# Sliding-window attention into a mixture of experts on one core: VectorE copy order, w2 rows in pairs, a fused sum and ReLU, and the order of tiles in the value matmuls

## The chip, the cores and the metric

The kernel runs on one core of one Trainium2 chip. The metric is the device time of one execution in microseconds (us); lower is better. Five engines take part: TensorE (PE; its weight loads are listed apart as PEld), VectorE (DVE), ScalarE (ACT), GpSimd (POOL) and SyncE (SP). Each has its own queue of instructions and works through it in order. POOL, SP and ACT also issue DMA transfers. Engines wait for each other by semaphores.

## The reference

The inputs are q, k and v for 4 batches, 8 heads, 768 positions and 64 values per head; routing weights for 3072 tokens and 4 experts; and for each expert w1 (512 x 1024) and w2 (1024 x 512). Cut to what matters:

```python
scores = scale * np.matmul(q, k.transpose(0, 1, 3, 2))
mask = np.where(retr, causal, causal & (is_sink | in_win))   # per head
a = softmax(np.where(mask, scores, -1e9))
x = np.matmul(a, v)             # laid out as 3072 tokens x 512
p = domain_probs / (domain_probs.sum(-1, keepdims=True) + 1e-09)
for e in range(E):
    h = np.maximum(x @ w1[e], 0.0)
    out += p[:, e:e + 1] * (h @ w2[e])
```

Heads 0, 2 and 6 attend to all earlier positions ("retrieval" heads); the other five attend to the first 4 positions and a window of 64.

## The kernel before, in words

**Attention in eight groups.** A group is one batch and one half of its 768 positions (`b`, `c`; group number `g` = 2b + c). `attention(b, c)` is a generator that emits the group's instructions step by step: transposed q and k, then per head `scores(h)` (key x query matmuls L659 into a PSUM bank, the exponential on ScalarE L677 into an `es` tile, and, except in group 0, a multiplication with a mask on VectorE L681) and `values(h)` or `values_r(h)` (value matmuls L785 and L713). The result goes to `xT`, the transposed tokens: 128 rows times 4 row blocks `ct` by 384 tokens. Heads with a window are scaled into `xT` by VectorE (L808) after a logarithm and an exponential on ScalarE (L803, L813). Retrieval heads go through `x_one` or `x_pair`, a transposition on TensorE (L762) and a copy by VectorE (L766, in `x_transposes`); in the later groups that copy is a DMA.

A retrieval head in the second half of a batch (`c` = 1) has four score tiles: the first two hold a diagonal block and are masked, the last two are not. `values_r` goes through them in the order in which `scores` made them (L705), and yields in the middle, after some 200 ns of matmuls (seven of them here).

**Instructions that wait their turn.** The order on each engine is written by hand. `later(op, g)` (L943) puts the scale L808 of a head into the list `behind`, due 1300 ns of estimated TensorE time later; `tick(ns)` (L946) moves that clock and emits what is due. In group 0 the end of the order is values of head 5 (row block 1), values of head 7 (row block 3), `x_transposes(6)` (all of row block 2), and then whatever is left behind. On VectorE this comes out as: scale of head 5, copy L766, scale of head 7.

**The experts.** Layer 1 multiplies w1 with the tokens, ReLU, and layer 2 multiplies with w2. Tokens of group 0 (three tiles of 128) and the first tile of group 1 go through `plain_steps`: for each expert L1027 takes 384 (or 128) columns of tokens against a 128 x 128 block of w1, over the row blocks in the order 0, 2, 1, 3. For the very first expert four PSUM banks are opened, and row blocks 0, 2, 1 are done for all four before row block 3. L1048 then multiplies with w2, 512 columns at a time.

The other tokens go in ten pairs of tiles through `pair_steps`. There layer 1 of the experts is plain (L1154, 256 columns), except for expert 3 always and expert 2 in the last three pairs: those take fewer products by a Strassen-Winograd scheme (`winograd_layer1`, L1183). In it `keep` copies a product to SBUF on ScalarE (L1193), and `add` adds a product in PSUM to a kept one on VectorE (L1199) and applies the ReLU in a second instruction (L1205); three such pairs for each expert and pair of tiles, 39 in all. Layer 2 of all pairs is L1290, with sums of w2 and of the hidden values made by VectorE (L967, L1134).

**The weights' way in.** All weights are cast from 4 to 2 bytes by DMAs that POOL issues: `load_w1(e, ...)` (L331, two DMAs of 64 partitions) and `load_w2(e)` (L339, one DMA). In `w2sb`, partition p holds rows p, 128 + p, 256 + p, ... of w2, one row of 512 to a block `ft`; the hidden unit that partition p of block `ft` of the hidden values stands for is therefore ft x 128 + p, and the weights of that block in layer 1 are 128 adjacent columns of `w1sb`. The loads go out in the order written in lines 491 to 527: w1 and w2 of expert 0, w1 of expert 1, then k and q for group 1 (L229), w2 of expert 1 and so on. `landed(x)` (L500) is a one-element copy on POOL that makes the instructions behind it wait until x has landed.

**Interleaving.** From group 1 on `moe_steps` emits the experts' work, and the loop at the end of the kernel inserts an attention step whenever a plan says so.

Of the kernel before, what the change touches and what calls it, by code (L numbers as in the profile page):

```python
# [9 lines left out]

# [3 lines left out]
ALU = mybir.AluOpType  # L14
# [4 lines left out]
def kernel(  # L19
# [33 lines left out]
    nc = tc.nc  # L53
    P = 128
# [276 lines left out]
    def load_w1(e, f0, f1):  # L331
        x = moe_w1[e].rearrange("(u c d) f -> u d c f", u=2, c=DMP)
        for u in range(2):
# [2 lines left out]
                in_=x[u, :, :, f0:f1],  # L336
            )

    def load_w2(e):  # L339
        gp.dma_start(  # L340
            out=w2sb[:, e * FTP : (e + 1) * FTP, :],
            in_=moe_w2[e].rearrange("(fo fi) d -> fi fo d", fi=P),
        )


    ONES = 0.0078125 * (1.0 + 15360.0 * 2.0**-23)
# [192 lines left out]
    def attention(b, c):  # L539
# [152 lines left out]
        def values_r(h):  # L692
# [9 lines left out]
            heads = heads.rearrange("p u (j x) -> p u j x", j=3)  # L702
            ps = heads[:, u if shared else 0, :, :]
            work = []
            for es, parts in es_of[h]:  # L705
                for t, o, q0, nq in parts:
                    for j in range(3):
                        x = j * P - q0
                        if 0 <= x < nq:
                            work.append((j, t, es[:, o + x : o + x + P]))  # L710
# [126 lines left out]
        if first:  # L837
# [17 lines left out]
            yield from both(scores(6), values(4))  # L855
            yield from both(scores(7), values(6))
            yield from values(5)
            yield from values(7)
            x_transposes(6)
            tick(LAG)  # L860
            small_things()
        else:
# [83 lines left out]
    def tick(ns):  # L946
        clock[0] += ns
        while behind and behind[0][0] <= clock[0]:
            behind.pop(0)[1]()
# [64 lines left out]
    def plain_steps(nt0, tiles, e, tokens, n0):  # L1014

        cols_n = tiles * P
        hs = hA[:, n0 : n0 + FTP * cols_n].rearrange("p (f x) -> p f x", f=FTP)
        require(nt0 // 3)
        x = tokens()
        ahead = 4 if nt0 == 0 and e == 0 else 1  # L1020
        for f0 in [0, *range(ahead, FTP)]:
            pss = {ft: bank() for ft in range(f0, f0 + (1 if f0 else ahead))}
            cts = (0, 2, 1, 3)

            def layer1(ft, n):
                ct = cts[n]
                nc.tensor.matmul(  # L1027
                    out=pss[ft][:, 0:cols_n],
                    lhsT=w1sb[:, e * DMP + ct, ft * P : (ft + 1) * P],
                    rhs=x[:, ct, :],  # L1030
                    start=(n == 0),
                    stop=(n == DMP - 1),
                )

            for ft in pss:
                for n in range(DMP - 1):
                    layer1(ft, n)
            for ft, ps in pss.items():
                layer1(ft, DMP - 1)
                nc.scalar.activation(  # L1040
                    out=hs[:, ft, :], in_=ps[:, 0:cols_n], func=AF.Relu
                )
                yield DMP * mm_ns(cols_n), 0.6
        for j in range(tiles):
            nt = nt0 + j
            ps_o = pO.tile([P, DM], FP32, name="pO", bufs=2)
            for ft in range(FTP):
                nc.tensor.matmul(  # L1048
                    out=ps_o,
                    lhsT=hs[:, ft, j * P : (j + 1) * P],  # L1050
                    rhs=w2sb[:, e * FTP + ft, :],
                    start=(ft == 0),
                    stop=(ft == FTP - 1),
                )
                if ft == FTP // 2 - 1:
                    yield FTP // 2 * mm_ns(DM), 1.4
            p_ap = p_sb[:, nt, e : e + 1]
            if e == 0:
                acc[nt] = acc_of(nt)
                nc.vector.tensor_scalar(  # L1060
                    out=acc[nt], in0=ps_o, scalar1=p_ap, scalar2=None, op0=ALU.mult
                )
            else:
                nc.vector.scalar_tensor_tensor(
                    out=acc[nt], in0=ps_o, scalar=p_ap, in1=acc[nt],
                    op0=ALU.mult, op1=ALU.add,
                )
            if e == E - 1:
                nc.sync.dma_start(out=out[nt * P : (nt + 1) * P, :], in_=acc[nt])
            yield FTP // 2 * mm_ns(DM), 1.4  # L1070
# [61 lines left out]
    def first_sum(e, n=1):  # L1132
# [2 lines left out]
            out=S1[:, k, :], in0=A21[:, k, :], in1=A22[:, k, :], op=ALU.add  # L1135
        )


    PSHARE = 1.57

# [5 lines left out]
    def pair_steps(nt0, nxt):  # L1146

        def plain_layer1(e):
            xs = scaled(e)
            for f0 in range(0, FTP, 2):  # L1150
                ps = bank()
                for f in range(2):
                    for ct in range(DMP):
                        nc.tensor.matmul(  # L1154
                            out=ps[:, f * PC : (f + 1) * PC],
                            lhsT=w1sb[:, e * DMP + ct, (f0 + f) * P : (f0 + f + 1) * P],
                            rhs=xs[:, ct, :],
                            start=(ct == 0),
                            stop=(ct == DMP - 1),
                        )  # L1160
# [15 lines left out]
        def winograd_layer1(e, x, y):  # L1176
# [18 lines left out]
            def block(n):  # L1195
                return blocks[:, n, e * HT : (e + 1) * HT, :]

            def add(n, ps, b):
                nc.vector.tensor_tensor(  # L1199
                    out=block(b),  # L1200
                    in0=ps.rearrange("p (f x) -> p f x", f=HT),
                    in1=kept[n].rearrange("p (f x) -> p f x", f=HT),
                    op=ALU.add,
                )
                nc.vector.tensor_scalar(  # L1205
                    out=block(b), in0=block(b), scalar1=0.0, scalar2=None, op0=ALU.max
                )

            def t(n):
# [337 lines left out]
```

The softmax here doesn't subtract the row's maximum and nothing guards it: scores larger than these inputs give would overflow.

## Time and profile before

| what | value |
|---|---|
| median of three runs | 378.41 us (377.46 to 378.68) |
| the profiled execution, its own time | 377.47 us |
| its span, first to last instruction | 375.8 us |
| mean granted TensorE clock | 1.000 |
| matmuls on L1154 (plain layer 1 of the pairs) | 864, 109.3 us busy |
| matmuls on L1290 (layer 2 of the pairs) | 1104, 133.4 us busy |
| first matmul of an expert (L1027) | at 20.37 us |
| transfers of w2, issue to landing, median of 4 | 12.5 us |
| packets in POOL's DMA queue | 86848 |

The profile is one execution of the program, taken by the hardware profiler. A row for a group of instructions gives its line, engine and operation, what it writes and reads, the shapes (partitions x elements, type) and how many there are, then its busy time and the mean length of one in ns, and last the idle time of the engine ahead of them with what ended most of it. A timeline row gives start and length in us. Matmuls are pipelined and each row of a matmul holds its full length, so matmuls overlap in the rows: the distance from one start to the next is the rate.

### The profile page before, as it was taken

How to read it: one execution, taken by the hardware profiler on the slowest of the kernel's cores; microseconds unless marked ns; L12 is line 12 of the kernel's file. 1: busy time of each engine (PE TensorE's matmuls, PEld its weight loads, DVE VectorE, ACT ScalarE, POOL GpSimd, SP SyncE). 2: the span in 40 equal slices, each digit the busy share in tenths (PEclk: the TensorE clock that was granted, in tenths of full speed). 3: DMA queues.
4: the chain of work that ended last, by engine and by line, in shares of the span. 5: the costliest groups of instructions: out<-in, count | busy, mean ns of one | idle time of the engine just before them, and what ended most of it. 6: DMA issues, size and time to landing. Idle time of an engine off the chain costs nothing.

```text
span 375.8 us, 10137 instructions
## 1 busy us (share of the span) xinstructions
PE 367.5 (98%) x4128; PEld 310.2 (83%) x4128; DVE 282.7 (75%) x620; ACT 227.8 (61%) x475; POOL 113.7 (30%) x155
## 2 busy tenths in 40 slices
PE   8889999999999999999999999999999999999996
PEld 4745466668998988999989898998899998999996
DVE  7774768697888679878758858967778868769572
ACT  3863478547785785765676955784777361450630
POOL 8934573882058038115601650320000000000000
PEclk9999999999999999999999999999999999999999
DMA  9999999999699599977904991951220300300101
GB/s 164 155 201 206 196 187 191 181 207 105 97 109 144 106 96 120 152 116 58 207 10 59 170 157 21 127 127 14 69 72 2 107 9 0 114 2 6 54 2 56
DMA packets 124771, 39.24 MB, mean 104 GB/s; under 512 B 113728, under 2 KB 118404, under 8 KB 124724
## 3 DMA queue, kind: packets, MB, share of 16 engines
q0 software_dynamic: 86848, 19.01, 59.1%
q1 hardware_dynamic: 36276, 19.18, 21.9%
q8 instruction: 32, 0.52, 0.6%
q10 hardware_dynamic: 1600, 0.39, 0.5%
q14 instruction: 15, 0.12, 0.1%
HBM read 44.89 MB, written 6.34 MB: 136 GB/s over the span
## 4 chain that ended last, share of the span: by engine, by line
PE 87%; DMA 7%; POOL 3%; DVE 2%; issue 0%; POOLq 0%
PE pO L1290 31%; PE pA L1154 25%; PE pO L1183 9%; DMA w2sb<-in_moe_w_dram 7%; PE pO L1048 6%; PE pA L659 5%; PE pA L1027 5%; PE pV L713 2%; PE pV L785 2%; PE pA L1183 2%; POOL vS L309 1%; POOL vR L303 1%; DVE xs L1112 1%; PE pA L1380 0%; POOL early L453 0%
## 5 line engine op out<-in xcount | busy, mean ns | idle before, releaser
L1290 PEld LDWEIGHTS <-hA 128*128 128x128 f16 x1104 | 104.9, 98 | 12.2
L1154 PE MATMUL pA<-xs,w1sb 128*128 128x256 f16 x864 | 109.3, 272 | 0.0
L1154 PEld LDWEIGHTS <-w1sb 128*128 128x128 f16 x864 | 80.7, 98 | 8.5
L1163 ACT ACTIVATE hA<-pA 128x512 f16<-128x512 f32 x108 | 64.4, 598 | 35.1 <-PE pA L1154 32.9
L1290 PE MATMUL pO<-w2sb,hA 128*128 128x256 f16 x640 | 76.7, 272 | 0.0
L677 ACT ACTIVATE es<-pA 128x384 f16<-128x384 f32 (+2 forms) x122 | 59.2, 511 | 27.1 <-PE pA L659 23.3
L305 POOL DMA_DIRECT2D vS<-in_v_dram x30 | 29.6, 989 | 111.7 <-PE pV L785 110.5
L1290 PE MATMUL pO<-tsb,hA 128*128 128x256 f16 x464 | 56.7, 272 | 0.0
L1112 DVE TENSOR_TENSOR xs<-xT,pB 128x1024 f16<-128x1024 f16 (+1 forms) x52 | 49.4, 969 | 1.2 <-DMA out_dram<-o 1.2
L967 DVE TENSOR_TENSOR hA<-hA 128x1024 f16<-128x1024 f16 x60 | 39.6, 684 | 0.4
L1040 ACT ACTIVATE hA<-pA 128x384 f16<-128x384 f32 (+1 forms) x64 | 22.2, 385 | 19.8 <-PE pA L1027 19.6
L1027 PE MATMUL pA<-xT,w1sb 128*128 128x384 f16 (+1 forms) x256 | 30.9, 273 | 1.3 <-DVE xT L766 0.8
L1048 PE MATMUL pO<-w2sb,hA 128*128 128x512 f16 x128 | 30.7, 379 | 0.3 <-DMA w2sb<-in_moe_w_dram 0.3
L1310 ACT COPY s<-pO 128x256 f32<-128x256 f32 x31 | 11.5, 372 | 27.7 <-PE pO L1290 21.9
L1027 PEld LDWEIGHTS <-w1sb 128*128 128x128 f16 x256 | 19.3, 98 | 10.2 <-issue 1.9
L808 DVE TENSOR_TENSOR xT<-pV,rc 64x384 f16<-64x384 f32 x37 | 20.5, 555 | 9.1 <-ACT rc L813 6.6
L1183 PEld LDWEIGHTS <-w1sb 128*128 128x128 f16 x416 | 26.3, 98 | 1.1 <-issue 0.2
L803 ACT ACTIVATE rc<-pV,eps 64x384 f32<-64x384 f32 x37 | 21.3, 576 | 6.5 <-PE pV L785 5.9
L1199 DVE TENSOR_TENSOR hA<-pO,s 128x512 f16<-128x512 f32 x26 | 17.9, 687 | 9.3 <-PE pO L1183 6.7
L681 DVE TENSOR_TENSOR es<-es,mS 128x384 f16<-128x384 f16 (+1 forms) x40 | 13.7, 343 | 13.4 <-ACT es L677 13.4
L659 PE MATMUL pA<-qT,kR 128*128 128x384 f16 (+2 forms) x120 | 22.9, 278 | 0.6 <-DVE kR L576 0.6
L1193 ACT COPY s<-pO 128x512 f32<-128x512 f32 x39 | 22.5, 585 | 1.4 <-PE pO L1183 1.2
(144 smaller groups left out, 498.2 us busy)
## 6 DMA issues: line engine op xcount, KB each, us to landing
pB<-p_rows SPq DMA_DIRECT2D x10, 512.0 KB
out_dram<-o SPq DMA_DIRECT2D x19, 256.0 KB
w1sb<-in_moe_w_dram POOLq DMA_DIRECT2D x8, 512.0 KB, 9.3
w2sb<-in_moe_w_dram POOLq DMA_DIRECT2D x4, 1024.0 KB, 12.5
vS<-in_v_dram POOLq DMA_DIRECT2D x30, 112.0 KB, 4.2
k_rows<-in_k_dram POOLq DMA_DIRECT2D x18, 128.0 KB, 5.6
q<-in_q_dram POOLq DMA_DIRECT2D x18, 128.0 KB, 6.4
vR<-in_v_dram POOLq DMA_DIRECT2D x24, 48.0 KB, 5.8
```

The source lines that it names most:

```text
L305: gp.dma_start(out=t[:, :, own_v(h)], in_=windows_of(v, b, h, c))
L659: nc.tensor.matmul(out=ps[:, o : o + nq], lhsT=key_tile(b, c, h, t), rhs=qTs[b, c][:, hp, q0 : q0 + nq], start=(n == 0 or not first), stop ...
L677: nc.scalar.activation(out=es[:, 0:cols], in_=ps[:, 0:cols], func=AF.Exp, scale=SC)
L967: nc.vector.tensor_tensor(out=out, in0=a, in1=b, op=ALU.subtract)
L1027: nc.tensor.matmul(out=pss[ft][:, 0:cols_n], lhsT=w1sb[:, e * DMP + ct, ft * P : (ft + 1) * P], rhs=x[:, ct, :], start=(n == 0), stop=(n = ...
L1048: nc.tensor.matmul(out=ps_o, lhsT=hs[:, ft, j * P : (j + 1) * P], rhs=w2sb[:, e * FTP + ft, :], start=(ft == 0), stop=(ft == FTP - 1),)
L1112: nc.vector.tensor_tensor(out=o, in0=xin, in1=pb.to_broadcast([P, DMP, n, P]), op=ALU.mult)
L1154: nc.tensor.matmul(out=ps[:, f * PC : (f + 1) * PC], lhsT=w1sb[:, e * DMP + ct, (f0 + f) * P : (f0 + f + 1) * P], rhs=xs[:, ct, :], start= ...
L1163: nc.scalar.activation(out=blocks[:, b0 : b0 + 2, k0 : k0 + 2, :].rearrange("p t f x -> p f t x"), in_=ps.rearrange("p (f t x) -> p f t x" ...
L1183: nc.tensor.matmul(out=ps[:, f * P : (f + 1) * P], lhsT=w[:, ct, f * P : (f + 1) * P], rhs=a[:, ct, :], start=(first and f == 0 and ct == ...
L1193: nc.scalar.copy(out=kept[n], in_=ps)
L1290: nc.tensor.matmul(out=ps, lhsT=a[:, k, :], rhs=b(k), start=(first and k == 0), stop=(k == KT - 1), skip_group_check=not first,)
```

## The change

Four edits, in all heads or experts that they name:

- **Copy order.** At the end of group 0, the scale of head 5 is taken out of the list `behind` and emitted after the copy of `x_transposes(6)`. On VectorE the order becomes copy L766, scale of head 5, scale of head 7. TensorE's and ScalarE's orders stay.
- **Two rows per partition.** For experts 0 and 1, w2 is loaded so that partition p of blocks 2m and 2m + 1 holds the adjacent rows 256m + 2p and 256m + 2p + 1. A piece of the transfer is then two rows, 4 KB read and 2 KB written, instead of one. The hidden units are thereby renumbered within each pair of blocks, and the weights of a block in layer 1 become every second one of 256 columns of `w1sb`. The loads of w1 stay as they are.
- **Fused sum and ReLU.** `add` in `winograd_layer1` is one instruction, min(sum, largest fp32 number) followed by max with 0, in place of two.
- **Unmasked tiles first.** For `c` = 1, `values_r` takes the third and fourth score tile first, and then the first and second.

```diff
+from concourse.dve_ops import TENSOR_ADD_SAT
...
+    def in_pairs(e):
+        return e < 2
+
+    def w1_tile(e, ct, ft):
+        x = w1sb[:, e * DMP + ct, :]
+        if in_pairs(e):
+            x = x[:, ft // 2 * 2 * P : (ft // 2 + 1) * 2 * P]
+            return x.rearrange("p (x j) -> p j x", j=2)[:, ft % 2, :]
+        return x[:, ft * P : (ft + 1) * P]
+
     def load_w2(e):
-        gp.dma_start(
-            out=w2sb[:, e * FTP : (e + 1) * FTP, :],
-            in_=moe_w2[e].rearrange("(fo fi) d -> fi fo d", fi=P),
-        )
+        x = w2sb[:, e * FTP : (e + 1) * FTP, :]
+        if in_pairs(e):
+            gp.dma_start(
+                out=x.rearrange("p (m j) d -> p m (j d)", j=2),
+                in_=moe_w2[e].rearrange("(m p j) d -> p m (j d)", p=P, j=2),
+            )
+            return
+        gp.dma_start(out=x, in_=moe_w2[e].rearrange("(fo fi) d -> fi fo d", fi=P))
...
-            for es, parts in es_of[h]:
+            tiles = es_of[h] if c == 0 else es_of[h][2:] + es_of[h][:2]
+            for es, parts in tiles:
...
             yield from values(5)
-            yield from values(7)
+            at_once = behind.pop()
+            v_steps = values(7)
+            yield next(v_steps)
             x_transposes(6)
+            at_once[1]()
+            yield from v_steps
             tick(LAG)
...
-                    lhsT=w1sb[:, e * DMP + ct, ft * P : (ft + 1) * P],
+                    lhsT=w1_tile(e, ct, ft),
...
-                            lhsT=w1sb[:, e * DMP + ct, (f0 + f) * P : (f0 + f + 1) * P],
+                            lhsT=w1_tile(e, ct, f0 + f),
...
+    LARGEST = 3.4028234663852886e38
...
             def add(n, ps, b):
-                nc.vector.tensor_tensor(
+                nc.vector._custom_dve(
+                    TENSOR_ADD_SAT,
                     out=block(b),
                     in0=ps.rearrange("p (f x) -> p f x", f=HT),
                     in1=kept[n].rearrange("p (f x) -> p f x", f=HT),
-                    op=ALU.add,
-                )
-                nc.vector.tensor_scalar(
-                    out=block(b), in0=block(b), scalar1=0.0, scalar2=None, op0=ALU.max
+                    s0=LARGEST,
+                    s1=0.0,
                 )
```

## The prediction

> **What bounds the kernel now.** I read the busy shares first, then TensorE's own waits, then the chain of waits around them in order of time, then the timeline of the two places where TensorE waits, then the transfers behind them, and last the rows of the operations that the change touches.
>
> ```profile
> ## 1 busy us (share of the span) xinstructions
> PE 367.5 (98%) x4128; PEld 310.2 (83%) x4128; DVE 282.7 (75%) x620; ACT 227.8 (61%) x475; POOL 113.7 (30%) x155
> ```
>
> TensorE is busy 98% of the span. Busy is not yet full rate, so I checked the rate: a piece of 32 matmuls over 128 columns takes 1.95 us with one matmul's 219 ns at its end, so they follow each other every (1.95 - 0.219)/31 = 55.8 ns, and eight of 256 columns take 0.87 us in the chain, 109 ns each. At 2.4 columns per ns (128 more columns, 53 ns more) that is the full rate of a granted clock of 1.000. Only instructions that make TensorE stand still, or make a matmul follow later than that, can move the end. This is the list of what TensorE's matmuls waited for (total us, times, longest):
>
> ```profile
> PE pA L1027 <- DVE xT L766: 0.8, 1, 0.8
> PE pV L713 <- DVE es L681: 0.6, 1, 0.6
> PE pA L1027 <- DMA w1sb<-in_moe_w_dram: 0.4, 1, 0.4
> PE pO L1048 <- DMA w2sb<-in_moe_w_dram: 0.3, 1, 0.3
> ```
>
> All four lie between 20 and 44 us; from 44 us to the tail TensorE's idle time is nil. The change aims at three of them. The chain of waits for 10 to 45 us (start, length, what):
>
> ```profile
> 13.13 12.54 DMA w2sb<-in_moe_w_dram
> ...
> 26.25 12.52 DMA w2sb<-in_moe_w_dram
> ...
> 38.81 1.02 PE pO L1048 x4
> ```
>
> So before 38.81 the chain is not TensorE's. It runs through the transfer of w2 of expert 0 into that of expert 1. The timeline at the two joints:
>
> ```profile
> 19.68 0.34 PE L762 MATMUL pV<-ident,x_pair 128*128 128x128 f16 x3
> 20.31 0.56 DVE L808 TENSOR_TENSOR xT<-pO,rc 64x384 f16<-64x384 f32 x1 [0.69 <-ACT rc L813]
> 20.37 0.32 PE L1027 MATMUL pA<-xT,w1sb 128*128 128x384 f16 x1 [0.36 <-DMA w1sb<-in_moe_w_dram]
> 20.90 0.56 DVE L766 CAST xT<-pV 128x384 f16<-128x384 f32 x1
> 21.52 5.45 PE L1027 MATMUL pA<-xT,w1sb 128*128 128x384 f16 x31 [0.82 <-DVE xT L766]
> 33.37 0.20 PEld L560 LDWEIGHTS <-q 128*64 128x64 f16 x6 [0.32 <-DMA q<-in_q_dram]
> ```
>
> **Copy order.** The copy L766 has its input at 20.02 (19.68 + 0.34), but stands behind the scale L808 of head 5, which waits for ScalarE until 20.31. In front, it runs at about 20.06 to 20.62; the scale follows at the spacing of these rows (20.90 - 20.31 = 0.59), 20.65 to 21.21. The scale of head 7 waited for ScalarE until 21.43 anyway, so it is not later. TensorE needs, in order, x rows 0, 2, 1: the first is there at 20.37, the second (the copy) at 20.65, the third (head 5's scale) at 21.25. Before, the third matmul ran at 21.52 + 0.16 = 21.68. Gain in the first layer: 21.68 - 21.25 = 0.43 us. No DMA is moved. Head 5's scale is what is now late.
>
> **Where that gain goes.** It must get past two landings. At 33.37 the weight load L560 waited for q, which lies in the Pool queue behind w1 of expert 1. Before 38.81 TensorE had taken in its 384-column matmuls by 38.35 (four from 37.70, 0.1625 us each; the list counts 0.28 of the rest as idle, as the last one drains until 38.53) and waited for w2 of expert 1. With all transfers unmoved, 0.43 us earlier only lengthens that wait from 0.46 to 0.89: **the copy order alone is worth 0.** What counts is how much earlier the two w2 transfers land.
>
> **w2 in pairs of rows.** The queue's packet count is one per contiguous piece: w2 of an expert is 1024 pieces of 1 KB (written), and becomes 512 of 2 KB. The bytes stay. The same queue, with 1 KB pieces of w2 of expert 0 (21 to 25 us), with 2 KB pieces of w1 (41.5 to 44.5) and with 1 KB pieces of w2 of expert 2 (47 to 50):
>
> ```profile
> DMA packets 743, 0.80 MB, mean 199 GB/s; under 512 B 13, under 2 KB 702, under 8 KB 742
> DMA packets 327, 0.63 MB, mean 210 GB/s; under 512 B 20, under 2 KB 20, under 8 KB 327
> DMA packets 623, 0.62 MB, mean 208 GB/s; under 512 B 15, under 2 KB 623, under 8 KB 623
> ```
>
> 1.049 MB at 199 is 5.27 us, at 210 it is 5.00, at 208 it is 5.04. So a transfer saves from 0.04 us (if 208 is what 1 KB pieces can do) to 0.27. The two rows for 1 KB disagree; between them I take 0.15 each, as the first is for expert 0 itself but has dips that need not come from the pieces. [...]
>
> Both transfers lie in one queue in order, so q lands 0.15 earlier and w2 of expert 1 0.30 earlier, at 38.48. TensorE, with 0.43 in hand and held to 0.15 of it at L560, is ready at 38.20 and starts L1048 at about 38.51: **gain 0.30**. On Pool the issue of w2 (908 ns, w1's of a quarter of the pieces 632) may shrink by up to 0.2; the queue is full then, so this is 0. Later landings (w1 of expert 2 seen at 46.97, needed at 47.80) move with the queue and keep their slack.
>
> **Unmasked tiles first.** L713 at 43.56 waited 0.57 for the masks on VectorE. In the new order its first seven matmuls take tiles 2 and 3 instead. By the row of three exponentials from 42.65 (1.47 us), tile 2 is ready at about 43.25 and tile 3 at 43.64; seven matmuls at 34 ns then end at about 43.76, against 43.56 + 0.24 = 43.80 before. I take **0.05**. From below: tile 3 is now the last needed, and a queued ScalarE row of 0.6 us before it would cost up to 0.5; from above: the whole 0.57. In the later groups other matmuls stand between, and TensorE's list has no wait for L681 or L677 there.
>
> **Fused sum and ReLU.** 39 instructions of 298 ns leave VectorE, 11.6 us:
>
> ```profile
> L1199 DVE TENSOR_TENSOR hA<-pO,s 128x512 f16<-128x512 f32 x26 | 17.9, 687 | 9.3 <-PE pO L1183 6.7
> L1205 DVE TENSOR_SCALAR hA<-hA 128x512 f16<-128x512 f16 x39 | 11.6, 298 | 1.3
> L1027 PEld LDWEIGHTS <-w1sb 128*128 128x128 f16 x256 | 19.3, 98 | 10.2 <-issue 1.9
> L557 PEld LDWEIGHTS pA<-early,hA 128*128 128x128 f32 x24 | 2.6, 144 | 1.3 <-POOL early L449 0.8 <-ACT es L677 0.3
> 73.86 1.95 PE L1027 MATMUL pA<-xT,w1sb 128*128 128x128 f16 x32
> ```
>
> The new operation is in no row. It reads the same PSUM bank, so between 687 ns (the plain add) and 985 (add and ReLU together); I take 687. Either way the end does not move: the cover is the matmuls of layer 1, and TensorE waits for none of these 39. Without cover (a product that goes on accumulating into the bank being read) the cost is what the add exceeds some 1.3 us of other matmuls by, so nothing up to 985 ns. Value **0**.
>
> **Strided weights.** w1 of experts 0 and 1 is now loaded every second column: 640 loads at L1154 under 109 ns matmuls, 64 at L1027 under 162 ns, 64 under 55.8 ns. No load in the trace is strided. A gain is excluded, as the load is already hidden. Lower end 0: the 98 ns of a load is latency, they pass every 55.8 ns. Upper end by the slowest load there is, the 4-byte one of L557: six of them in 0.67 us, (0.67 - 0.144)/5 = 105 ns apart. That still hides under 109 and 162 and costs 64 x (105 - 55.8) = 3.1 us. If nothing overlapped, 144 ns each, it would be 640 x 35 + 64 x 88 = 28 us. I take 0, since only the step changes and the type (2 bytes) and the 128 columns stay those of the 98 ns row. [...]
>
> **Sum.** 0.30 + 0.05 + 0 + 0 = 0.35 us off the profiled execution's 377.47 (span 375.8 and 1.7 around it, which stay). That execution is the lowest of its kind; the median is 378.41, so I predict 378.41 - 0.35 = 378.06, about **378.1**. What a measurement can tell from no change is some 0.3%, 1.13 us.
>
> **Rivals.** (1) *The packets do not matter*: 208 GB/s is the limit for either size, the w2 landing stays, and copy order is absorbed there. For it: w2 of expert 2. Against: w2 of expert 0. 378.41 - 0.08 - 0.05 = 378.3. (2) *The transfers gain more*: if a piece costs by its share of engine time (121% at 1 KB, 112% at 2 KB in those windows), a transfer saves 8% of 5.27, 0.43 us, two 0.86; then the copy's 0.43 passes L560, TensorE is ready at 37.92 as w2 lands (38.78 - 0.86), and with all of 0.57 at L713 it is 1.43: 377.0. Against: bytes per second differ by 5%, not 8. (3) *The strided load outlasts a 128-column matmul*: at L1027 with 128 columns, from 74 us on, price 3.1 - 0.35 = 2.75, so 381.2; it decides once a load takes more than 55.8 + 1500/64 = 79 ns, which the 98 ns duration does not rule out. (4) *A new wait at L713* for the last exponential in each of the four second groups, at most 4 x 0.5 = 2: 380.1; against it, the matmuls between.
>
> **Chances.** Forecast 0.38, (1) 0.17, (2) 0.23, (3) 0.18, (4) 0.04. The likeliest one's own range is 377.6 to 378.5 (0.04 to 0.27 per transfer, 0 to 0.3 at L713). The range takes in (2) and half the way to (3): 376.9 to 380.2. Faster 0.24 (case 2, and a little of the forecast), same 0.54, slower 0.22 ((3) and (4)).
>
> **What would show it.** L766 ahead of L808 on VectorE, TensorE's third L1027 near 21.25; 1024 packets fewer in the queue; L1048 of expert 1 near 38.5, still just behind its transfer; L1205 gone; L1154 still 109 ns apart and the 128-column L1027 still 1.95 us for 32. It is wrong if those 32 take more than 2.5 us, or if L1048 of expert 1 starts at 38.8 or before 38.2.

## The result, and the profile after

The changed kernel takes 378.12 us (median of 4 runs, 377.49 to 378.32) against 378.36 (4 runs, 377.46 to 378.68) for the kernel before, measured alongside it: a ratio of 0.9995, interval 0.9974 to 1.0016. No difference can be told, and the forecast was 378.1. The profiled execution took 378.03 us with a span of 376.3; the one of before took 377.47 with 375.8. So in this pair of traces the changed kernel is the longer one, though nearly every stage starts earlier in it. A later measurement with more runs gave 377.96 (11 runs, 377.51 to 379.93) against 377.50 (15 runs): 1.0010, interval 0.9997 to 1.0024. Two of the eleven executions of a later kernel, `pairs_rounds`, the profiled one among them, took 545.34 and 639.65 us at granted clocks of 0.657 and 0.560 and are left out of everything below.

In the changed kernel the line numbers are: L676 scores, L694 exponential, L698 mask, L732 value matmuls, L785 the copy and L827 the scale on VectorE, L1050 and L1071 the plain layers 1 and 2, L1179 layer 1 of the pairs, L1208 the Winograd products, L1225 the fused instruction.

The page of the changed kernel, busy shares and queues (packets, MB, share of 16 engines):

```profile
span 376.3 us, 10100 instructions
PE 368.0 (98%) x4128; PEld 310.6 (83%) x4128; DVE 271.6 (72%) x581; ACT 228.0 (61%) x475; POOL 113.2 (30%) x155
q0 software_dynamic: 85824, 19.01, 59.7%
```

VectorE loses 39 instructions and 11.1 us of work; TensorE is at 98% as before. POOL's queue has 86848 - 85824 = 1024 packets fewer at the same bytes. Its list of TensorE's waits (total us, times, longest):

```profile
PE pV L732 <- ACT es L694: 1.3, 2, 1.0
...
PE pO L1071 <- DMA w2sb<-in_moe_w_dram: 0.5, 1, 0.5
PE pA L1050 <- DVE xT L827: 0.3, 1, 0.3
PE pA L1050 <- DMA w1sb<-in_moe_w_dram: 0.3, 1, 0.3
```

The 0.8 us for the copy has become 0.3 us for the scale, and the wait for w2 has grown from 0.3 to 0.5. The wait for the masks is gone, but one for the exponential stands in its place: of the 1.3 us, 1.0 was there before (in group 0), 0.31 is new. The timeline of the changed kernel at the first matmul of an expert:

```profile
20.06 0.56 DVE L785 CAST xT<-pV 128x384 f16<-128x384 f32 x1 [0.44 <-PE pV L781]
20.27 0.72 PE L1050 MATMUL pA<-xT,w1sb 128*128 128x384 f16 x2 [0.25 <-DMA w1sb<-in_moe_w_dram]
20.65 0.56 DVE L827 TENSOR_TENSOR xT<-pO,rc 64x384 f16<-64x384 f32 x1
21.26 0.97 PE L1050 MATMUL pA<-xT,w1sb 128*128 128x384 f16 x5 [0.27 <-DVE xT L827]
```

The copy runs first, the scale directly behind it, and the third matmul starts at 21.26 (21.68 before). And the chain of waits of the changed kernel further on:

```profile
13.14 12.28 DMA w2sb<-in_moe_w_dram
...
26.00 12.55 DMA w2sb<-in_moe_w_dram
...
38.59 1.02 PE pO L1071 x4
```

The chain still runs through both transfers of w2, and L1071 of expert 1 still starts just behind its transfer, now at 38.59 instead of 38.81. The first transfer is 0.26 us shorter from issue to landing, the second 0.03 longer. So 0.22 us are gained at this point, and 0.24 at the first pair of tiles (L1179 starts at 87.90, before at 88.14). 0.14 of that is lost between 103 and 119 us, and at the end only 0.09 is left: VectorE's last instruction ends at 373.11 instead of 373.20. From there to the end of the span it is 3.2 us, where it was 2.6 before; that is where the longer span comes from. It is not chance. The last 32 matmuls and the next-to-last sum on VectorE, before:

```profile
370.92 1.95 PE L1380 MATMUL pA<-tsb,hA 128*128 128x128 f16 x32
372.09 0.29 DVE L1387 TENSOR_TENSOR o<-pA,s 128x128 f32<-128x128 f32 x1 [0.54 <-PE pA L1380]
```

and in the changed kernel:

```profile
370.83 1.95 PE L1405 MATMUL pA<-tsb,hA 128*128 128x128 f16 x32
372.35 0.29 DVE L1412 TENSOR_TENSOR o<-pA,s 128x128 f32<-128x128 f32 x1 [0.89 <-PE pA L1405]
```

The matmuls are the same, but the sum starts 1.52 us after the first of them instead of 1.17, and the span ends 5.47 us after it instead of 4.84. The runs below show the longer end in every kernel with the fused instruction and in no other.

The place of the loss, value matmuls of the second half of batch 1 (group 3), in the timeline of before:

```profile
116.92 1.47 ACT L677 ACTIVATE es<-pA 128x512 f16<-128x512 f32 x3 [0.49 <-PE pA L659]
...
118.19 0.38 PE L713 MATMUL pV<-vR,es 128*128 128x65 f16 x7
```

and in that of the changed kernel:

```profile
116.68 1.47 ACT L694 ACTIVATE es<-pA 128x512 f16<-128x512 f32 x3 [0.49 <-PE pA L676]
...
117.95 0.52 PE L732 MATMUL pV<-vR,es 128*128 128x65 f16 x7
```

Three exponentials in a row end at 118.15. In the old order the seven matmuls that start at 117.95 (0.24 earlier than before) would not touch the last of them; in the new order some of the seven need it, and they take 0.52 us instead of 0.38, although the row, being one group of seven, lists no wait.

### The profile page after: what moved, and what is told of

Same layout as the page of the kernel before. It is cut to its first block, busy times and chain, and to the rows that moved or that the text cites. A ratio compares the mean times of both kernels' runs of the same rounds, so it can differ in the third digit from the quotient of the medians.

```text
span 376.3 us, 10100 instructions
## 1 busy us (share of the span) xinstructions
PE 368.0 (98%) x4128; PEld 310.6 (83%) x4128; DVE 271.6 (72%) x581; ACT 228.0 (61%) x475; POOL 113.2 (30%) x155
## 3 DMA queue, kind: packets, MB, share of 16 engines
q0 software_dynamic: 85824, 19.01, 59.7%
HBM read 44.89 MB, written 6.34 MB: 136 GB/s over the span
## 4 chain that ended last, share of the span: by engine, by line
PE 87%; DMA 7%; POOL 3%; DVE 1%; issue 0%; ACT 0%; POOLq 0%
PE pO L1315 31%; PE pA L1179 25%; PE pO L1208 9%; DMA w2sb<-in_moe_w_dram 7%; PE pO L1071 6%; PE pA L676 5%; PE pA L1050 5%; PE pV L732 2%; PE pV L804 2%; PE pA L1208 2%; POOL vS L310 1%; POOL vR L304 1%; DVE xs L1135 1%; PE pA L1405 0%; POOL early L470 0%
## 5 line engine op out<-in xcount | busy, mean ns | idle before, releaser
L1179 PE MATMUL pA<-xs,w1sb 128*128 128x256 f16 x864 | 109.3, 273 | 0.0
L1179 PEld LDWEIGHTS <-w1sb 128*128 128x128 f16 x864 | 80.7, 98 | 8.5
L694 ACT ACTIVATE es<-pA 128x384 f16<-128x384 f32 (+2 forms) x122 | 59.2, 511 | 27.3 <-PE pA L676 23.5
L1050 PE MATMUL pA<-xT,w1sb 128*128 128x384 f16 (+1 forms) x256 | 31.1, 273 | 0.7 <-DVE xT L827 0.3
L1071 PE MATMUL pO<-w2sb,hA 128*128 128x512 f16 x128 | 30.7, 379 | 0.5 <-DMA w2sb<-in_moe_w_dram 0.5
L827 DVE TENSOR_TENSOR xT<-pV,rc 64x384 f16<-64x384 f32 x37 | 20.5, 555 | 9.8 <-ACT rc L832 7.3
L1050 PEld LDWEIGHTS <-w1sb 128*128 128x128 f16 x256 | 19.4, 98 | 9.7 <-issue 1.5
L1208 PEld LDWEIGHTS <-w1sb 128*128 128x128 f16 x416 | 26.3, 98 | 1.1 <-issue 0.2
L1225 DVE CUSTOM_DVE_ANT_0 hA<-pO,s 128x512 f16<-128x512 f32 x26 | 17.7, 689 | 12.5 <-PE pO L1208 8.8
L698 DVE TENSOR_TENSOR es<-es,mS 128x384 f16<-128x384 f16 (+1 forms) x40 | 13.7, 344 | 15.0 <-ACT es L694 15.0
L676 PE MATMUL pA<-qT,kR 128*128 128x384 f16 (+2 forms) x120 | 22.9, 278 | 0.6 <-DVE kR L593 0.6
```

Source lines behind the costliest of these rows:

```text
L676: nc.tensor.matmul(out=ps[:, o : o + nq], lhsT=key_tile(b, c, h, t), rhs=qTs[b, c][:, hp, q0 : q0 + nq], start=(n == 0 or not first), stop ...
L694: nc.scalar.activation(out=es[:, 0:cols], in_=ps[:, 0:cols], func=AF.Exp, scale=SC)
L1050: nc.tensor.matmul(out=pss[ft][:, 0:cols_n], lhsT=w1_tile(e, ct, ft), rhs=x[:, ct, :], start=(n == 0), stop=(n == DMP - 1),)
L1071: nc.tensor.matmul(out=ps_o, lhsT=hs[:, ft, j * P : (j + 1) * P], rhs=w2sb[:, e * FTP + ft, :], start=(ft == 0), stop=(ft == FTP - 1),)
L1179: nc.tensor.matmul(out=ps[:, f * PC : (f + 1) * PC], lhsT=w1_tile(e, ct, f0 + f), rhs=xs[:, ct, :], start=(ct == 0), stop=(ct == DMP - 1),)
L1208: nc.tensor.matmul(out=ps[:, f * P : (f + 1) * P], lhsT=w[:, ct, f * P : (f + 1) * P], rhs=a[:, ct, :], start=(first and f == 0 and ct == ...
```

## The experiments

The questions: is the gain 0.22 us a matter of the packets (my theory) or of when the transfers happen to land; is the copy order really worth nothing alone; and what does the order of tiles cost? All runs compute the full result. To compare executions whose first transfers land at different times, I use distances between two starts. "First layer" is the distance from the start of the normalization of the pair's values (`x_pair`, VectorE) to the first layer-2 matmul of expert 0: 7.54 us in the trace of before. "Group 3" is the distance from the start of layer 2 of the first pair (L1290, at 103.85 us before) to the start of layer 1 of the next pair (L1154, at 118.62), around the place shown above: 14.77 us before, 14.91 after. "End" is the distance from the first of the last 32 matmuls to the end of the span: 4.84 us before, 5.47 after.

### The kernel before once more (`before_again`)

No edit.

> The kernel before once more, to see how much one profiled execution differs from another at the marks that the other runs are read by: first layer 1 of expert 0 in full flow at 21.52 us, q of group 1 landed at 33.13, L1048 of expert 1 at 38.81, first L1154 at 88.14, last matmul piece at 370.92. If these marks move by more than 0.1 us without any edit, differences of 0.2 us between traces say nothing. I expect 0.05 us or less on TensorE's and VectorE's marks, up to 0.2 us on landings of transfers, and up to 0.7 us between the last VectorE instruction and the end of the span (2.6 us before, 3.2 in the changed kernel).

Measured: 377.85 us, span 376.1 (378.15 for the other run of the same kernel beside it). The times agree, but not the stages. The first matmul of an expert starts at 21.26 instead of 20.37. The transfers as POOL saw them land, in the first trace of before:

```profile
20.29 0.18 POOL L502 COPY seen<-w1sb 1x1 f16<-1x1 f16 x1 [1.46 <-DMA w1sb<-in_moe_w_dram]
25.80 0.23 POOL L502 COPY seen<-w2sb 1x1 f16<-1x1 f16 x1 [3.76 <-DMA w2sb<-in_moe_w_dram]
33.15 0.18 POOL L502 COPY seen<-q 1x1 f16<-1x1 f16 x1 [6.01 <-DMA q<-in_q_dram]
```

and in this one:

```profile
21.17 0.18 POOL L502 COPY seen<-w1sb 1x1 f16<-1x1 f16 x1 [2.34 <-DMA w1sb<-in_moe_w_dram]
26.98 0.20 POOL L502 COPY seen<-w2sb 1x1 f16<-1x1 f16 x1 [4.06 <-DMA w2sb<-in_moe_w_dram]
34.20 0.18 POOL L502 COPY seen<-q 1x1 f16<-1x1 f16 x1 [5.88 <-DMA q<-in_q_dram]
```

Identical code lands its weights 0.9 to 1.2 us apart, and the layer 2 of expert 1 starts 0.38 us apart (38.81, 39.19). My expectation was missed by a wide margin: a difference of 0.22 us between two traces is below what one execution differs from the next. The distances hold: first layer 7.55, group 3 14.78, end 4.83.

### The copy order alone (`copy_only`)

```diff
-            yield from values(7)
-            x_transposes(6)
+            at_once = behind.pop()
+            v_steps = values(7)
+            yield next(v_steps)
+            x_transposes(6)
+            at_once[1]()
+            yield from v_steps
```

> Only the copy order. Theory (what the forecast rests on): the first layer gains 0.43 us (third L1027 at 21.25 instead of 21.68) and the wait for w2 of expert 1 swallows all of it, so that matmul row stays at 38.81 +- 0.1 with a gap ahead of it about 0.4 us longer, and the first L1154 stays at 88.1. Rival: the copy order itself brought the 0.22 us that the changed kernel shows there (38.59), because the landing of w2 has nothing to do with its pieces; then it reads 38.6 here too.

Measured: 377.34 us, span 375.6. First layer 7.13, so 0.41 us shorter. But the second half of my expectation fell. Part of the chain of waits of this run:

```profile
20.79 0.56 DVE xT L766
21.38 0.57 DVE xT L808
21.99 1.96 PE pA L1031 x11
...
38.09 0.76 PE pA L1031 x4
38.84 0.86 PE pO L1052 x4
```

No transfer is in it: here w2 of expert 1 had landed, and layer 2 followed layer 1 without a wait. From the start of expert 0's layer 2 to expert 1's it is 11.56 us, against 12.01 before and 12.21 after, both of which contain a wait for w2. `later_t` below has the old order and no wait for q or w2 there either: it needs 19.16 us from `x_pair` to layer 2 of expert 1, `copy_only` 18.69. So the copy order's gain reaches this point when q and w2 land in time, and is swallowed, as in the changed kernel's first trace, when they don't.

### The pairs of rows alone (`pairs_only`, `pairs_rounds`)

The edits to `load_w2`, `w1_tile` and the two places that use it, nothing else.

> Only w2 of experts 0 and 1 in pairs of rows, with the strided weights. Theory: w2 of expert 0 lands 0.25 us earlier (25.42 in the changed kernel, 25.67 before), L1048 of expert 1 starts near 38.6, as with the whole change, since TensorE is ready at 38.35 without the copy order too; so pairs alone bring all of the 0.22 us. Rival: the landings vary by that much from run to run, and the start is anywhere between 38.5 and 38.9. The strided loads cost nothing by the changed kernel's rows (98 ns, 128-column matmuls 1.95 us for 32): the same is expected here.

Measured in one execution: 380.59 us, span 378.9. Group 0 was late (first layer 1 at 21.32) and w1 of expert 2 landed at 48.89 instead of 46.97. Between 44 and 90 us TensorE waited 1.3 us for w1 (of experts 2 and 3) and 0.4 for w2; another 0.5 us went near 250 us. Nothing in the edit touches the load of w1, and `tiles_only`, with the old loads, has it as late as 48.31. So the same kernel was timed in more executions:

> The kernel with only w2 of experts 0 and 1 in pairs of rows, again and timed in five rounds, since its one look gave 380.59 us where the kernel before gave 378.15 on the same chip and where the whole change gave 378.12. Theory: the 2 us are one slow stretch of transfers (w1 of expert 2 landed at 48.89 us instead of 46.97, with TensorE waiting), as w1 of expert 0 landed 0.9 us apart in two executions of the same kernel; so five rounds give a median within 0.4 us of the kernel before (377.9 to 378.8). Rival: the strided weights or the larger pieces cost 2 us unless the other three edits come with them; then the median is 380 or more.

Measured: 377.52 us (median of 9) against 377.46 (33 runs): 1.0003, interval 0.9992 to 1.0014. None of the nine is above 378.55, so the 2 us of the first execution are not the kernel's. The edit is worth nothing that can be measured in the time; the strided loads cost nothing either, unless a gain of the loads hides it.

For the transfer itself, the time from the landing of w1 of expert 0 to that of w2 of expert 0, by POOL's copies: with one row to a piece 5.51, 5.81, 5.31, 5.54, 6.34, 5.69, 5.47 and 5.70 us in eight executions; with two rows 5.36, 5.08, 5.24 and 5.23 in four. The middle values are 5.62 and 5.24. That speaks for some 0.4 us less: only one of the eight (5.31) is below the longest of the four. But the eight spread over 1 us, so the size is uncertain.

### The order of tiles alone (`tiles_only`), and the change without it (`no_tiles`)

```diff
-            for es, parts in es_of[h]:
+            tiles = es_of[h] if c == 0 else es_of[h][2:] + es_of[h][:2]
+            for es, parts in tiles:
```

> Only the order of tiles in the value matmuls. Theory from the changed kernel's trace: nothing gained at group 1 (L1048 that follows at 43.8, within 0.05), and 0.14 us lost at group 3, where the seven value matmuls near 118.2 take 0.52 us instead of 0.38 as they wait for the exponential of the last tile; so the pair that begins at 149.34 before begins at 149.5. Rival: the 0.14 is a side effect of the other edits having moved the attention steps, and is not there alone: 149.34.

Measured: 379.0 us, span 377.3. Group 3 is 14.91, as in the changed kernel. The rest of its extra time lies elsewhere: a late w1 (0.8 us of waits) and a wait of 0.7 us near 249 us that is told of below.

> The whole change without the order of tiles in the value matmuls. Theory: the seven value matmuls of group 3 take 0.38 us again instead of 0.52, so the stretch from the second to the third stage of the pairs (103.6 to 118.6) is 14.77 us as before, not 14.91, and the time is 0.13 us lower than the whole change, 377.9 to 378.1 in the median; nothing is lost at group 1. Rival: the masks then hold up group 1 by 0.2 us or more (L713 there waited 0.57 for VectorE before), and the time is that of the whole change or higher.

Measured: 377.45 us, 1.0002, interval 0.9993 to 1.0011, span 375.7. Group 3 is 14.78 again. Over all runs the distance is 14.77 to 14.78 in every kernel of before's order (`before_again`, `copy_only`, `pairs_only`, `no_tiles`, `ct_major`, `halves` and both `reorder` runs) but `later_t`, which waits for q there, and 14.91 in every one of the new order (the change twice, `tiles_only`). So the new order costs 0.14 us there, each time. What it gains is in group 1, where the changed kernel has:

```profile
42.43 1.47 ACT L694 ACTIVATE es<-pA 128x512 f16<-128x512 f32 x3 [0.21 <-PE pA L676]
43.08 0.65 PE L732 MATMUL pV<-vR,es 128*128 128x65 f16 x7 [0.31 <-ACT es L694]
43.57 0.81 PE L1071 MATMUL pO<-w2sb,hA 128*128 128x512 f16 x3
```

Layer 2 at 43.57 is 4.98 us behind the start of expert 1's layer 2 (38.59). Before, it was 43.80 - 38.81 = 4.99. The matmuls start 0.48 us earlier, but four of the seven run and the other three then stand until the exponential of the second unmasked tile is done: 0.01 us gained.

`no_tiles` also shows where a gain at the front goes in the time. Its first pair starts at 87.73 us (88.14 before) and its last 32 matmuls at 370.53 (370.92), so it is still 0.39 us ahead there. But its end is 5.17 us, 0.33 more than before's 4.84, and the span comes out 0.06 shorter. The end is 4.83 or 4.84 in the ten traces without the fused instruction, among them `copy_only`, `pairs_only` and `tiles_only`, and 5.17, 5.47 and 5.25 in the three with it (`no_tiles` and the change twice). In these three the next-to-last sum on VectorE starts 1.51 to 1.53 us after the first of the 32 matmuls, in the ten 1.16 or 1.17. The fused instruction was not run alone, so a combination of it with the copy order or the pairs isn't excluded. Why the sum is late is open. One thing differs nearby: the last 8 KB packet of the DMA queue that the page calls instruction (q14) lies 2.8 to 3.0 us ahead of the end in the three and 23 to 30 us in the ten. It starts behind the late sum, so it can't be what delays that; what it does to the output transfers was not tested.

### The first layer row block by row block (`ct_major`), and the weights in halves (`halves`)

With the copy order, the opening of the first expert goes through the row blocks outermost, so that the four banks' work on block 0 and block 2 covers the scale that is late:

```diff
-            for ft in pss:
-                for n in range(DMP - 1):
+            for n in range(DMP - 1):
+                for ft in pss:
                     layer1(ft, n)
```

> Copy order, and besides the first layer of expert 0 takes row block 0 for all four open banks, then row block 2, then 1, instead of 0, 2, 1 bank by bank, so that the four matmuls of row block 0 fill the wait for the copy and the scale. Theory: the first layer is done 0.6 to 0.7 us earlier than with the copy order alone for the same landing of w1 (the 30 matmuls then run without the stop of 0.27 and 0.3), and all of it is swallowed at the landings of q and of w2 of expert 1, so the time is that of the kernel before within 0.3 us. Rival: TensorE's own order is what sets this stretch, and the time is 0.6 us or more lower.

Measured: 377.36 us, 0.9996, interval 0.9987 to 1.0005. First layer 6.82, another 0.3 off, although TensorE waits 0.6 us for w1 in it; in `reorder_copy` and `halves` below, where that wait is gone, the first layer takes 6.32, 0.8 less than with the copy order alone. The first 32 matmuls run without a gap:

```profile
21.06 5.61 PE L1031 MATMUL pA<-xT,w1sb 128*128 128x384 f16 x32 [0.61 <-DMA w1sb<-in_moe_w_dram]
```

Yet layer 2 of expert 1 starts at 38.78, since TensorE now waits 0.3 us for q. `halves` adds to this kernel that every load of w1 and w2 goes out as two transfers, so that the first half can be used sooner:

```diff
-    load_w1(0, 0, F)
+    load_w1(0, 0, F // 2)
+    load_w1(0, F // 2, F)
```

> As the kernel before it in this list (copy order, row block by row block), and every load of w1 and w2 in two halves, by hidden units 0 to 511 and 512 to 1023, in the same order. Pieces of w1 are then half as long (512 columns), those of w2 stay one row. Theory: the first four blocks of a layer need only the first half, which lands some 2.5 us before the whole, so TensorE's waits for w1 of expert 0, and for w2 of expert 1 (0.46 us before) go: first L1027 at about 20.05 without a stop, L1048 of expert 1 at 37.6 to 38.2 instead of 38.8, and the time 0.8 to 1.4 us lower than before (377.0 to 377.6), with less spread. Rival: the second halves are then waited for just as long, because the queue's bytes set the end of this stage and not the order of what lands; then the time is within 0.3 us of before. A second rival: 1 KB pieces of w1 slow the queue, and it is higher.

Measured: 377.96 us (377.27 to 380.39), 1.0019, interval 1.0002 to 1.0035. The first matmul starts at 19.87 and layer 2 of expert 0 at 25.59, earlier than in any other run. It brings nothing: the interval lies just above 1. The list of TensorE's waits of this run begins

```profile
PE pV L566 <- DMA q<-in_q_dram: 1.4, 1, 1.4
```

and layer 2 of expert 1 starts at 38.98. Time won ahead of q turns into waiting for q. In this run what POOL's queue has to carry up to q sets the end of this stage, in the traces of before and of the change what it has to carry up to w2 of expert 1.

### w2 of expert 1 ahead of k and q (`reorder`, `reorder_copy`)

If the queue's order sets it, the weights can go first. The attention of group 1 then has to begin later:

```diff
+    load_w2(1)
+    landed(w2_of(0))
     load_triples(k, k16, 0, 1, 0, HP)
     load_triples(q, qt16, 0, 1, 0, HP)
-    landed(w2_of(0))
-    load_w2(1)
...
-    plan = {1: (1.06 * UNIT, 3.5 * UNIT)}
+    plan = {1: (1.5 * UNIT, 3.5 * UNIT)}
```

`reorder_copy` is the same with the copy order and the row blocks outermost.

> The kernel before with w2 of expert 1 put ahead of the first halves of k and q of group 1 in the Pool queue, and group 1's attention begun later (at 1.5 instead of 1.06 of an expert's estimated work). None of the four edits is in it. Theory: w2 of expert 1 then lands about 1.9 us earlier (0.39 MB less ahead of it at 205 GB/s), near 36.7 to 37.5, before TensorE asks for it; the waits at q and at w2 of expert 1 (0 to 0.2 and 0.46) go and the time is 0.3 to 0.7 us lower, if group 1's attention still fits behind. Rival: group 1's attention, pressed into less time, makes TensorE wait for ScalarE and VectorE by as much or more between 42 and 62 us; then the time is that of before or up to 1 us higher.

> The same with the copy order and the first layer taken row block by row block. Theory (the landings were what swallowed the copy order): with w2 of expert 1 out of the way the first layer's 0.4 to 1.0 us comes through to the pairs, so the first piece of the pairs starts 0.4 us or more before that of the run without it for equal landings of w1, and the time is 0.4 to 0.9 us lower than that run's. Rival: it is swallowed again by the next landing (w2 of expert 0, or k and q, or w1 of expert 2), and both are equal within 0.2 us.

Measured: 387.26 us, 1.0255 (1.0236 to 1.0274), and 387.0, 1.0249 (1.0236 to 1.0262). Layer 2 of expert 1 did start earlier, at 37.58 and 37.00. But the price follows at once. TensorE in `reorder`:

```profile
52.60 1.44 PE L1027 MATMUL pA<-xT,w1sb 128*128 128x384 f16 x4 [5.38 <-DMA w1sb<-in_moe_w_dram]
```

and POOL:

```profile
38.47 0.18 POOL L502 COPY seen<-q 1x1 f16<-1x1 f16 x1 [10.47 <-DMA q<-in_q_dram]
42.62 1.28 POOL L334 DMA_DIRECT2D w1sb<-in_moe_w_dram  x2
...
52.59 0.18 POOL L502 COPY seen<-w1sb 1x1 f16<-1x1 f16 x1 [4.33 <-DMA w1sb<-in_moe_w_dram]
```

The loads of w1 of expert 2 stand behind the wait for q in POOL's order. They go out at 42.62 (37.32 before) and land at 52.59 (46.97), 5 us after TensorE wants them. Behind the stop comes a second price. TensorE's granted clock in `reorder`, 1.00 up to 51 us, is 0.50 from 52 to 58 us and 1.00 again from 59 us (mean over the run 0.99, before 1.000); the four matmuls above take 1.44 us, four alike before take 0.81. The time is 9.7 us higher, where the rival had at most 1. In the traces `reorder_copy` is 0.84 us ahead of `reorder` at the first pair, but 0.78 of that is an earlier landing of w1 of expert 2 (51.81); the times differ by 0.26 with overlapping intervals, so whether the first layer's gain is kept when w2 is early stays open.

### The late transfer near 250 us (`later_t`)

Some executions lose 0.5 to 1.1 us at 249 us, where a Winograd product waits for VectorE (in `tiles_only` the list names ScalarE). There VectorE's line that sums tokens (L1112 in before) waits for a transfer of transposed tokens, long enough to delay TensorE in `ct_major` and not in `copy_only`. First `ct_major`, then `copy_only`:

```profile
247.58 1.29 DVE L1116 TENSOR_TENSOR xs<-xT,pB 128x512 f16<-128x512 f16 x2 [3.17 <-DMA xT<-x_pair]
```

```profile
245.83 1.29 DVE L1116 TENSOR_TENSOR xs<-xT,pB 128x512 f16<-128x512 f16 x2 [1.52 <-DMA xT<-x_pair]
```

My guess was that the six transposing transfers of the next group's k and q, on the same queue, push it back. They were moved one head later:

```diff
-                if n == 3 and more and g > 1:
+                if n == 4 and more and g > 1:
```

> The kernel before with the six transposing DMAs of the next group's k and q issued one head later, behind the transposing DMA of x_pair instead of ahead of it. Theory on the spread: the runs of 378 us and more (7 of the 33 runs of the kernel before in the last comparison) are those in which x_pair's transfer, sixth behind those on SP's queue, lands so late near 246 us that VectorE's L1112 and then TensorE's L1183 wait (1.1 us of TensorE in one trace, 0 in another); so here no run, or one of eleven, is at 378 or above, and the median is 0 to 0.2 us lower. Rival: those runs are late for another reason (landings before 62 us), and the share stays near a fifth; or the later transposes are now waited for by the next group, and all runs are slower.

Measured: 380.64 us, 1.0085 (1.0071 to 1.0098). The next groups' scores now wait for q (1.3 us), and the loss near 250 us stayed at 1.1. The guess fell; what makes that transfer late in some executions is open, and so is which one it is: at the same line `pairs_only` names an output transfer (2.61 us) and `later_t` one of q (3.11).

### The change once more (`change_again`)

No edit to the changed kernel.

> The whole changed kernel again, in five rounds, for a closer interval and a second trace of it. Theory: all four edits together are worth less than the landings differ from one execution to the next, so the ratio is 0.9985 to 1.0010 with 1.000 inside the interval, and the 0.22 us at L1048 of expert 1 of the first trace does not return as such (anything from 38.4 to 39.2); the 0.14 us lost at the value matmuls of group 3 does return (14.91 us from the second to the third stage of the pairs, 14.77 before). Rival: the change is a small steady gain of 0.3 us (0.9992), as forecast, and the interval shows it.

Measured: 377.96 us, 1.0010 (0.9997 to 1.0024), span 377.2 with the loss near 250 us in it (TensorE waited 0.8 us). First layer 7.11, group 3 14.91, both as in the first trace; the end is 5.25, long again. Layer 2 of expert 1 started at 38.68 without a wait for w2, where the first trace waited 0.5.

## Why the prediction was right, and where its steps were not

**The time** was right: no difference that can be told, in the forecast's direction within noise in one measurement and against it in the other. Four small terms were added up, and the largest possible sum (1.43 us, rival 2) was barely above what can be told, so the time alone says little about the terms. The traces show 0.4 us gained by the copy order where q and w2 are in time, 0.14 lost by the order of tiles and 0.3 to 0.6 lost at the end.

**Copy order: right to 0.02 us in the first layer.** Forecast 0.43; measured 7.54 to 7.11 twice and 7.12 and 7.13 in the two other kernels that have it and keep the first layer's order (7.54 to 7.57 in all with the old one). The order of the two landings on VectorE, the spacing of 0.59 and the third matmul at 21.25 (21.26) all held.

**"The copy order alone is worth 0" was too strong.** It is the step that failed in its condition: the working held one execution's landings fixed. With w2 of expert 1 late, as in the trace of before, the gain is swallowed; in `copy_only`, `no_tiles` and `change_again` w2 was there and nothing was swallowed. In the times it still can't be seen: 1.0002 for `no_tiles`, whose longer end takes back 0.33, and 0.9996 for `ct_major`.

**w2 in pairs: the first transfer is probably shorter; what reaches TensorE is not settled.** Forecast 0.30 at layer 2 of expert 1, measured 0.22: the issue of the second transfer came 0.25 us earlier (forecast 0.15), and that transfer was no shorter (forecast 0.15). But the spread of identical code at this point, 0.38, is larger than the term, so that 0.22 lies near 0.30 is luck. Rival 2's time, 377.0, is ruled out: it would be a ratio of 0.9963, and the interval begins at 0.9974. Its 0.43 us for one transfer, though, is nearer to what w2 of expert 0 shows (5.24 against 5.62 us) than the forecast's 0.15. Rival 1, that packets do not matter, can't be told from the forecast by time; these landings speak against it.

**Unmasked tiles first: wrong in size and, over the whole kernel, in sign.** Forecast 0.05 gained in group 1 and nothing later, as "other matmuls stand between". Measured: 0.01 in group 1 and 0.14 lost in group 3. In group 3 other matmuls do stand between, eight of layer 2 in 1.04 us and two of the scores, but five score matmuls come in a burst ahead of them, ScalarE works through three exponentials until 118.15, and the value matmuls begin at 117.95 and need the third. That is rival 4's mechanism, in one of the four groups and at 0.14 instead of 0.5 each. I had looked only for waits that the list named in the old order; the question was which of the next instruction's inputs would be the last one made.

**Fused sum and ReLU: the price was right, the value of 0 probably not.** 687 ns was taken; the costliest groups on the changed kernel's page have 689:

```profile
L1225 DVE CUSTOM_DVE_ANT_0 hA<-pO,s 128x512 f16<-128x512 f32 x26 | 17.7, 689 | 12.5 <-PE pO L1208 8.8
```

11 us of VectorE's time go and the pairs get no shorter: from the first pair to the last 32 matmuls it is 282.80 us in `no_tiles` (87.73 to 370.53) and 282.78 before (88.14 to 370.92). No matmul waited for it: from 44 us on the list of TensorE's waits is empty in the first trace of before and in that of the change. But the prediction took what follows the last matmuls as unchanged, without a term for it, and the three traces with this instruction take 0.33 to 0.63 us longer there. No rival had that.

**Strided weights: right at 0, rival 3 ruled out.** The weight loads in the same groups, half of them strided, and then TensorE's timeline for 128 columns, experts 0 and 1 strided, expert 2 plain:

```profile
L1050 PEld LDWEIGHTS <-w1sb 128*128 128x128 f16 x256 | 19.4, 98 | 9.7 <-issue 1.5
```

```profile
73.63 1.95 PE L1050 MATMUL pA<-xT,w1sb 128*128 128x128 f16 x32
...
77.14 1.95 PE L1050 MATMUL pA<-xT,w1sb 128*128 128x128 f16 x32
...
80.66 1.95 PE L1050 MATMUL pA<-xT,w1sb 128*128 128x128 f16 x32
```

With half of the group strided its mean is 98 ns, as it was with none (L1027 before, 98 ns); for the pairs (L1179, 640 of the 864 loads strided) it is 98 ns too. 32 matmuls over 128 columns take 1.95 us behind strided and plain loads alike, so they follow each other every 55.8 ns as before.

No version that was run beats both kernels by more than its interval; the lowest, `ct_major`, is at 0.9996 (0.9987 to 1.0005).

## What to carry to other kernels

When a stage waits for transfers, take its marks from two executions of the same kernel before you trust a term of a few tenths of a us: here the landings moved by 0.9 to 1.2 us in identical code, more than any of the four edits was worth (0.43 at most), while distances between instructions on the engines repeated to 0.03 us (first layer 7.54 to 7.57) and settled what the copy order and the order of tiles do. Take such a distance for the end of the span too, before a longer end is put down to chance (4.83 or 4.84 us in ten traces here, 5.17 to 5.47 in three). A reordering of inputs should be judged by which input is made last, not by the wait that the profile names for the present order: the new order of tiles removed a named wait of 0.57 us and lost 0.14 elsewhere. Time won ahead of a shared queue can be lost again at the next thing that the queue brings (in `halves` the first matmul of an expert came at 19.87 us, 20.37 before, and TensorE then waited 1.4 us for q), and moving one transfer forward moves the issues that stand behind a wait in the same order (in `reorder` those of w1 of expert 2 went from 37.32 to 42.62).

## What was not expected of the hardware

- Transfers issued within 0.02 us of the same time (POOL's issues of w1 at 11.92 and 11.93, of w2 at 13.13 in both) landed 0.9 to 1.2 us apart in two executions of identical code (w1 of expert 0 at 20.29 and 21.17, w2 at 25.80 and 26.98); whether both ran on one chip isn't known.
- The time from VectorE's last instruction to the end of the span was 2.55 or 2.56 us in ten traces and 2.89, 2.97 and 3.19 in the three with the fused instruction, though the same instructions stand there.
- After a stop of 5.4 us TensorE's granted clock was 0.50 for some six us in `reorder` (52 to 58 us), where it was 1.00 in the trace of before.
- The wait near 250 us took 0.5 to 1.1 us of TensorE's time in `ct_major`, `tiles_only`, `pairs_only`, `later_t` and one execution of the change, and nothing in eight others, with the same instructions around it.
